# MLP unit 0's gate in two pieces, and the query fold over six blocks of 120 rows loaded later

## The chip, the cores and the metric

The kernel runs on one core of one Trainium2 chip. The metric is the device time of one execution in microseconds (us), as the median of several runs. The engines are TensorE (PE, with its weight loads shown apart as PEld), VectorE (DVE), ScalarE (ACT), GpSimd (POOL) and SyncE (SP, which here only issues DMAs).

## What is computed

The input x has 2048 tokens of 640 features. It is normalised (layernorm), and two branches read the normalised xn: a linear attention with 32 heads of 20 features, and a gated MLP with 1536 hidden features. The output is x + attention + MLP.

```python
qkv = (xn @ wqkv)                      # 640 -> 3 x 640, split in 32 heads of 20
pq, pk = q @ w_phi, k @ w_phi          # per head 20 x 20
phi_q = concat(softmax(pq), softmax(-pq)); phi_k likewise
kv = phi_k^T v;  z = sum(phi_k)        # per head, over all tokens
o  = (phi_q kv) / (phi_q z + 1e-6);  A = o @ wo
h  = silu(xn @ w1) * (xn @ w3);  B = h @ w2
out = x + A + B
```

## The kernel before

The tokens are 16 tiles of 128. A tile t is normalised in place in `x_tok` and transposed into `xnT` (features on the partitions, tokens along the free axis). Tiles 0 to 3 are transposed on PE with an identity matrix (`xn_transpose`), tiles 4 to 15 by DMA transposes that SP issues (`loads`), one of 160 KB for each tile.

The feature map is folded into the projections. Wqp is wq times a block-diagonal matrix that holds w_phi for each head, and Wkp is the same with wk; with them xn @ Wqp gives pq at once. For the fold, wq and wk stand transposed in `wqkT` (five chunks of 128 rows each, one chunk list for wq and one for wk). Each is brought by one DMA transpose of 640x640 from DRAM. The block-diagonal chunks `BDc` are made on POOL from `phi_s` and the mask `GM`. 128 rows aren't a whole number of heads of 20, so a chunk touches 7 or 8 heads and neighbouring chunks overlap by one head; `fold_mm` makes one output chunk `dc` of Wqp or Wkp in six matmuls of 140, 140, 80, 80, 140 and 140 columns, which accumulate into two PSUM banks of 320 columns. The fold of wk (`which` = 1) runs between 17 and 20 us of the profile, the fold of wq (`which` = 0) as one `fold_mm` after each of the token tiles 9 to 13.

The MLP is 48 units (`mlp`): unit n = 12 b + fc takes the 512 tokens of block b and 128 hidden features. A unit is five matmuls for the gate (w1), five for the up-projection (w3), each 128x128 weights on 512 tokens, a tanh on ACT, and two DVE operations. Attention takes each tile's keys (`k_tile`: ten matmuls of 320 columns, two exponentials) and its values (`v_tile`). Then come the key norms, the key-value sums, the queries, and the output tiles (`outs`), which add both branches.

The order of all instructions is made by a planner before the program is built. There are 14 streams (`norms`, `transposes`, `fold_k`, `attention`, `k_norms`, `loads`, `key_values`, ..., `mlps`, `outs`); each yields its next step, or None while a condition on the table `done` doesn't hold. The planner keeps a clock for each engine (`P.free`), a cost for every instruction and a landing time for every DMA, and in each turn commits the step that can start first by these counts; on a tie the stream that stands earlier in the list wins, so `attention` goes ahead of `mlps`. For a step with PE work the start is the larger of PE's free time + 0.15 and the time at which its inputs are there (`P.ready`), to which 0.25 (`SLACK`) is added after 20 us. What comes out is a fixed list for each engine; on the chip every engine works its list in order and waits on semaphores. A DMA transpose of less than 500 KB counts as 1.28 us of SP and lands, if no earlier transfer holds it back, 0.5 us + its bytes at 280 GB/s + 1.6 us after its issue begins; a plain DMA counts as 0.45 us of SP:

```python
if "T" == o.part:
    self.free[o.eng] = t + (1.28 if o.cost < 5e5 else o.cost / 105e3)
self.bus = max(self.bus, t + 0.5) + o.cost / (280e3 if o.part else 305e3)
```

SP's list before: the first loads (x tiles 0 to 3, part of wv, the first third of w1 and w3), `phi_s`, the transpose of wk, x tiles 4 to 15 in three loads, the transpose of wq, then the DMA transposes of tiles 4 to 7, the second third of w1 and w3, the transposes of tiles 8 to 15, the last third of w1 and w3, wo. All PE, ACT, DVE and POOL instructions show as line L102 and all DMA issues as L114, so the text goes by tile names: `w_s` stands for w1, w2 and w3, `t` for t1, `v` for v2.

Of the kernel before, what the change touches and what calls it, by code (L numbers as in the profile page):

```python
# [3 lines left out]
ACT = mybir.ActivationFunctionType  # L4
ALU = mybir.AluOpType
# [4 lines left out]
D = 640  # L10
H = 32
DH = 20
# [237 lines left out]
def bass_parallel_sum__linear_kernel_hedgehog__glu_gated_swiglu__prompt_kernel(  # L250
# [37 lines left out]
    GM = new("GM", [128, DC, H], bf)  # L288
    phi_s = new("phi_s", [128, DC, DH], bf)
    BDc = new("BDc", [128, DC, 8 * DH], bf)  # L290
    bst = new("bst", [128, T, 15], f32)
    mv = new("mv", [128, T, 2], f32)
    rstd = new("rstd", [128, T, 2], f32)
# [25 lines left out]

    RE = region(T * 2 * D * 2 + 96)  # L320
    ekt = new("ekt", [128, T * 2 * D + 48], bf, RE)
    hT3 = new("hT3", [128, FC, 512], bf, RE)
    w2_s = new("w2_s", [128, FC, D], bf, RE + 12288)
    eq = [new(f"eq{i}", [128, NG * 128], bf, (RKV, RE + 27648)[i // 2] + 2816 * (i % 2)) for i in range(4)]
# [5 lines left out]
    oT = new("oT", [128, DC, S], bf, RV)  # L330

    RW = region(12800)
    wqkT = new("wqkT", [128, 2 * DC, D], bf, RW)
    KVc = new("KVc", [128, NG * 64], bf, RW)
    half = new("half", [128, 2, 660], f32, RW + 1408)
    Sq = new("Sq", [128, 4, 72], f32, RW + 6688)
# [55 lines left out]
    def memset(eng, o, v):  # L392
        P.op(eng, "memset", [o], [], (o, v), cost=0.15 + free(o) / 960)
# [8 lines left out]
    out_t = out.rearrange("b (t p) d -> p (b t) d", p=128)  # L402
    wqkv_t = A_wqkv.rearrange("(c p) n -> p c n", p=128)
    phi_t = A_w_phi.rearrange("h d f -> (h d) f").rearrange("(c p) f -> p c f", p=128)
    w1_t = B_w1.rearrange("(c p) f -> p c f", p=128)
    w3_t = B_w3.rearrange("(c p) f -> p c f", p=128)

# [7 lines left out]
    def first_loads():  # L415
        def part_wv(eng, a, b):
            P.dma(eng, wv[:, :, a:b], wqkv_t[:, :, 2 * D + a:2 * D + b])

        P.dma("SP", x_tok[:, 0, 0:320], x_t[:, 0, 0:320])
        P.dma("ACT", x_tok[:, 1, :], x_t[:, 1, :])  # L420
        P.dma("SP", x_tok[:, 0, 320:D], x_t[:, 0, 320:D])
        load_x(2, 3)
        part_wv("ACT", 0, VCUT)
        part_wv("SP", VCUT, D)
        load_x(3, 4)
        w13(0, 512)
        P.dma("SP", phi_s[:], phi_t)
        P.dma("SP", wqkT[:, DC:2 * DC, :], A_wqkv[:, D:2 * D], True)
        load_x(4, 8)
        load_x(8, 12)  # L430
        load_x(12, 16)
        P.dma("SP", wqkT[:, 0:DC, :], A_wqkv[:, 0:D], True)


    def consts():
        memset("DVE", t1[:, 2, 0:128], 0.0)
        memset("DVE", warm[:], 0.0)
        memset("DVE", bst[:, :, 12:14], 0.0)
        memset("DVE", bst[:, :, 14:15], D * EPS)
        act(warm[:], warm[:], ACT.Exp)  # L440
        memset("POOL", ident[:], 0.0)
        select(ident[:], 0, [[-1, 128]], 1, ALU.not_equal, 1.0)
        memset("POOL", GM[:], 1.0)
        select(GM[:], 0, [[128, DC], [-DH, H]], 1, ALU.is_ge, 0.0)
        select(GM[:], DH, [[-128, DC], [DH, H]], -1, ALU.is_gt, 0.0)
        memset("POOL", mhalf[:], -0.5)
        memset("POOL", M3[:, 0:3], 1.0)
        select(M3[:, 0:3], 0, [[-40, 3]], 1, ALU.is_ge, 0.0)
        select(M3[:, 0:3], 40, [[40, 3]], -1, ALU.is_gt, 0.0)
        memset("POOL", ekt[:, T * 2 * D:T * 2 * D + 48], 1.0)  # L450
# [77 lines left out]
               phi_s[:, c, :].unsqueeze(1).to_broadcast([128, n, DH]),  # L528
               GM[:, c, h0:h1 + 1].unsqueeze(2).to_broadcast([128, n, DH]), ALU.mult)

    def fold_mm(which, dc, k, eng=None):
        first = [True, True]
        for e in range(DC):
            h0, h1 = heads_of_chunk(e)
            lo, hi = DH * h0, DH * (h1 + 1)
            for q in range(2):
                a, b = max(lo, 320 * q), min(hi, 320 * q + 320)
                if a < b:
                    mm(bank(k + q, b - a, a - 320 * q), wqkT[:, which * DC + e, 128 * dc:128 * dc + 128],
                       BDc[:, e, a - lo:b - lo], first[q], e == DC - 1 or (q == 0 and e == 2), True)  # L540
                    first[q] = False
        dst = (Wqp, Wkp)[which]
        o = dst[:, dc, :].rearrange("p (b c) -> p b c", c=320)
        if eng:
            copy(eng, o, bank2(k, 320))
        else:
            evac(o, bank2(k, 320))
# [134 lines left out]
    def mlp(b, fc, k, cut=DC, dc=None):  # L682
        n = nmlp[0] % 3
        nmlp[0] += 1
        for w, kk in ((w1_s, k), (w3_s, k + 1)):
            for i in range(DC):
                if kk > k and i == cut:
                    held.add(k // 2)
                    fold_mm(1, dc, banks(2), "ACT")
                    held.discard(k // 2)  # L690
                mm(bank(kk), w[:, i, fc * 128:(fc + 1) * 128], xnT[:, i, b * 512:(b + 1) * 512],
                   i == 0, i == DC - 1)
            if kk == k:
                act(th[:, n, :], bank(k), ACT.Tanh, 0.5)
                stt(t1[:, n, :], th[:, n, :], 1.0, bank(k), ALU.add, ALU.mult)
        stt(hT[b][:, fc, :], t1[:, n, :], 0.5, bank(k + 1), ALU.mult, ALU.mult)

    finish = []

# [31 lines left out]
                       default=0.0)  # L731
        return min((k for k in range(0, 8, n) if k // 2 not in held), key=free_at)

    done = dict.fromkeys(("w", "ln", "t", "f", "k", "n", "kv", "v", "u", "qp", "qn", "qd", "q", "o", "h", "v0", "bd"), 0)

    def norms():
        yield lambda: (first_loads(), consts())
        yield lambda: act_sum(1, ACT.Copy, mv[:, 1, 0:1], scale=-1.0 / D)
        yield lambda: (ln_half(0, 0), ln_half(0, 1), ln_rstd(0, 1))
        yield lambda: act_sum(1, ACT.Square, mv[:, 1, 1:2], mv[:, 1, 0:1])  # L740
        yield lambda: (ln_apply(0, 0, 256), ln_apply(0, 256, D))
        done["ln"] = 1
        yield lambda: act_rstd(1)
        yield lambda: (ln_half(2, 0), ln_half(2, 1))
        yield lambda: ln_apply(1)
        done["ln"] = 2
        yield lambda: ln_rstd(2, 1)
        while done["t"] < 2:
            yield None
        yield lambda: ln_apply(2)  # L750
        done["ln"] = 3
        yield lambda: (ln_half(3, 0), ln_half(3, 1), ln_rstd(3, 1))
        yield lambda: ln_apply(3)
        done["ln"] = 4
        while done["t"] < 4:
            yield None
        yield lambda: memset("DVE", v_heads(v2[:].rearrange("p t n -> p (t n)"))[:, :, :, DH], 1.0)
        yield block_diag
        done["bd"] = 1
        todo = []  # L760
        for t in range(4, T + 2, 2):
            if t == T or t > done["k"] + 8:
                for u in todo:
                    yield lambda u=u: ln_apply(u)
                    done["ln"] = u + 1
                todo = []
            if t == T:
                break
            while t > done["k"] + 8:
                yield None  # L770
            yield lambda t=t: ln_stats(t, 2)
            for u in todo:
                yield lambda u=u: ln_apply(u)
                done["ln"] = u + 1
            todo = [t, t + 1]

    def fold_k():
        while done["u"] < 2:
            yield None
        for dc in range(1, DC - 1):  # L780
            yield lambda dc=dc: fold_mm(1, dc, banks(2), "ACT")
        done["f"] = 1

    done["w"] = 4
# [22 lines left out]
    def loads():  # L807
        while done["t"] < 4:
            yield None
        for t in range(4, T):  # L810
            while done["ln"] <= t:
                yield None
            yield lambda t=t: P.dma("SP", xnT[:, :, t * 128:(t + 1) * 128], x_tok[:, t, :], True)
            done["t"] = t + 1
            if t == 7:
                yield lambda: w13(512, 1024)
                done["w"] = 8
        yield lambda: w13(1024, 1536)
        done["w"] = 12

    def attention():
# [4 lines left out]
        for t in range(4):  # L826
            while done["t"] <= t:
                yield None
            k = banks(2)
            held.add(k // 2)  # L830
            for q in range(2):
                for i in range(DC):
                    if t == 0 and q == 1:
                        while done["t"] < 2:
                            yield None
                    yield lambda t=t, q=q, i=i, k=k: v_part(t, q, i, k)
                    done["v0"] += 1
            yield lambda t=t, k=k: v_store(t, k)
            held.clear()
        while done["u"] < 3:  # L840
            yield None
        for t in range(T):
# [4 lines left out]
            if t >= 4:  # L847
                yield v(t)
            if 9 <= t < 14:
                yield lambda dc=t - 9: fold_mm(0, dc, banks(2))  # L850
        yield lambda: P.dma("SP", wo_s[:], A_wo.rearrange("(c p) d -> p c d", p=128))
        done["v"] = 1

# [60 lines left out]
    CUTS = {1: (3, 0), 2: (0, DC - 1)}  # L914

    def mlps():
        for b in range(NB):
            for fc in range(FC):
                while done["t"] < 4 * b + 4 or done["w"] <= fc or b == 2 and done["t"] < T or b == 3 and not done["kv"]:
                    yield None  # L920
                n = 12 * b + fc
# [122 lines left out]
```

## Time and profile before

| what | value |
| --- | --- |
| median of 3 runs | 268.06 us (267.88 to 269.06) |
| profiled execution, its own time | 268.03 us |
| its span, first to last instruction | 266.3 us |
| PE busy | 261.8 us (98%) |
| DVE, ACT, POOL busy | 169.2, 98.3, 97.9 us |
| granted TensorE clock | 1.000 |

The span leaves out about 1.7 us of the execution's own time. A matmul's record has a modelled end, so busy PE time says when PE had work, and the spacing of matmuls is read from the starts in the timeline. Some matmul records are missing. The profile's rows that carry the argument stand in the prediction.

### The profile page before, as it was taken

To read this page: it belongs to the slowest core of one execution; us is meant where nothing else is said; L and a number is where in the kernel's file an instruction comes from. 1 tells how busy PE (TensorE), PEld (TensorE's weight loads), DVE (VectorE), ACT (ScalarE), POOL (GpSimd) and SP (SyncE) were. 2 spreads that over 40 slices of the span, in tenths; PEclk is the share of its full clock that TensorE was granted. 3 is DMA by queue.
4 is the path that set the end of the run, shared out by engine and by line. 5 is a ranking of instruction groups with operands and counts; after the bars stand their busy time and mean duration, and the time that the engine had idled before them with its cause. 6 is when DMAs were issued, how large, how long until landed. Compare 5 with 4: busy or idle time off the path is not lost.

```text
span 266.3 us, 4843 instructions
## 1 busy us (share of the span) xinstructions
PE 261.8 (98%) x1962; PEld 161.9 (61%) x1981; DVE 169.2 (64%) x293; ACT 98.3 (37%) x196; POOL 97.9 (37%) x136
## 2 busy tenths in 40 slices
PE   8999999999999999999999999999999999999996
PEld 7666777775444575455545555554677777777773
DVE  4469989974998957769788888888723121212112
ACT  5578998878222206344344333442100000000000
POOL 4313459999461332734265544444200000000000
PEclk9999999999999999999999999999999999999999
DMA  7999896600007059247335356365422412131211
GB/s 224 279 319 195 121 252 158 240 2 0 0 0 111 0 157 242 54 55 106 79 79 81 80 99 109 84 70 93 101 67 84 102 58 89 52 98 52 85 38 49
DMA packets 63510, 27.73 MB, mean 104 GB/s; under 512 B 50560, under 2 KB 63488, under 8 KB 63488
## 3 DMA queue, kind: packets, MB, share of 16 engines
q1 hardware_dynamic: 62544, 26.66, 44.2%
q10 hardware_dynamic: 944, 0.77, 0.9%
q8 instruction: 15, 0.25, 0.4%
q14 instruction: 7, 0.06, 0.1%
HBM read 12.81 MB, written 2.62 MB: 58 GB/s over the span
## 4 chain that ended last, share of the span: by engine, by line
PE 98%; issue 0%; DVE 0%
PE PS L102 98%; DVE xres L102 0%; DVE t L102 0%; DVE bst L102 0%; DVE warm L102 0%
## 5 line engine op out<-in xcount | busy, mean ns | idle before, releaser
L102 PE MATMUL PS<-xnT,w_s 128*128 128x512 bf16 x466 | 105.5, 379 | 0.9 <-issue 0.2
L102 PEld LDWEIGHTS PS<-xnT,w_s 128*128 128x128 bf16 x480 | 45.9, 98 | 51.4 <-ACT xnT L102 0.3
L102 PE MATMUL PS<-w_s,hT 128*128 128x320 bf16 (+2 forms) x384 | 54.9, 299 | 0.0
L102 DVE TENSOR_TENSOR xres<-PS,xres 128x640 bf16<-128x640 f32 (+2 forms) x17 | 13.4, 786 | 57.7 <-PE PS L102 57.7
L102 ACT ACTIVATE th<-PS 128x512 f32<-128x512 f32 x48 | 29.2, 609 | 51.4 <-PE PS L102 51.4
L102 POOL TENSOR_TENSOR ekt<-ekt,rS 128x640 bf16<-128x640 bf16 x32 | 39.5, 1272 | 19.8 <-DVE rS L102 19.8
L102 PEld LDWEIGHTS PS<-w_s,hT 128*128 128x128 bf16 x384 | 37.1, 98 | 15.1
L102 DVE SCALAR_TENSOR_TENSOR t<-th,PS 128x512 bf16<-128x512 f32 x48 | 32.6, 679 | 17.5 <-ACT th L102 16.8
L102 DVE SCALAR_TENSOR_TENSOR hT<-t,PS 128x512 bf16<-128x512 bf16 x48 | 33.0, 688 | 5.4 <-DVE t L102 0.5
L102 ACT ACTIVATE eq<-PS 128x600 bf16<-128x600 f32 (+1 forms) x72 | 23.7, 424 | 27.9 <-PE PS L102 27.9
L102 PE MATMUL PS<-wv,xnT 128*128 128x320 bf16 (+2 forms) x160 | 24.6, 300 | 0.0
L102 PE MATMUL PS<-wo_s,oT 128*128 128x320 bf16 (+2 forms) x159 | 24.3, 299 | 0.1
L102 PE MATMUL PS<-Wkp,xnT 128*128 128x320 bf16 x160 | 23.7, 299 | 0.0
L102 PE MATMUL PS<-Wqp,xnT 128*128 128x512 bf16 (+1 forms) x156 | 23.3, 297 | 0.2
L102 DVE TENSOR_REDUCE S<-ekt 128x64 f32<-128x1280 bf16 x16 | 23.0, 1440 | 0.0
L102 POOL TENSOR_TENSOR eq<-eq,rq 128x600 bf16<-128x600 bf16 (+1 forms) x32 | 22.6, 728 | 1.2
L102 ACT ACTIVATE ekt<-PS 128x640 bf16<-128x640 f32 x32 | 20.5, 705 | 3.6 <-PE PS L102 3.6
L102 POOL TENSOR_TENSOR half<-eq 128x660 f32<-128x660 bf16 x14 | 19.0, 1357 | 4.4 <-ACT eq L102 4.4
L102 POOL TENSOR_TENSOR rq<-rq,Sq 128x32 f32<-128x32 f32 x16 | 4.0, 253 | 44.6 <-DVE rq L102 40.5
L102 PEld LDWEIGHTS PS<-wv,xnT 128*128 128x128 bf16 x160 | 15.3, 98 | 6.5 <-ACT xnT L102 0.4
L102 PEld LDWEIGHTS PS<-wo_s,oT 128*128 128x128 bf16 x160 | 15.4, 98 | 6.2
L102 PEld LDWEIGHTS PS<-Wqp,xnT 128*128 128x128 bf16 x160 | 12.8, 98 | 10.2
(57 smaller groups left out, 180.5 us busy)
## 6 DMA issues: line engine op xcount, KB each, us to landing
w_s<-in_B_w_dram SPq DMA_DIRECT2D x6, 640.0 KB, 6.0
xres<-in_A_x_dram SPq DMA_DIRECT2D x16, 160.0 KB, 2.4
out_dram<-xres SPq DMA_DIRECT2D x15, 160.0 KB, 1.8
x_tok<-in_A_x_dram SPq DMA_DIRECT2D x3, 640.0 KB, 6.0
w_s<-in_B_w_dram SPq DMA_DIRECT2D x1, 1920.0 KB, 7.6
wo_s<-in_A_wo_dram SPq DMA_DIRECT2D x1, 800.0 KB, 7.1
wv<-in_A_wqkv_dram ACTq DMA_DIRECT2D x1, 560.0 KB, 5.0
x_tok<-in_A_x_dram SPq DMA_DIRECT2D x2, 160.0 KB, 4.7
```

Source lines behind the costliest of these rows:

```text
L102: o = _Op(eng, lambda: m(*args, **kw), r, w, cost)
```

## The change

Three things change together.

1. MLP unit 0 is no longer one step. Its gate is computed for the first 384 tokens as soon as three tiles are transposed (`mlp_first`), and for the last 128 tokens, with the rest of the unit, once the fourth is (`mlp_rest`). The pair of PSUM banks is held in between.
2. The query fold takes six blocks of rows at a stride of 120 (six whole heads; the last block has 40 rows of use, two heads). wq is loaded transposed in six DMA transposes of 128 columns of wqkv each (`load_wqT`); the last 8 rows of each block are not used. The block-diagonal matrix for it is `BD6`, made on POOL in one operation after unit 0 (`block_diag6`) from `phi_6`, which two more small loads bring, and the mask `GM6`. `fold_q` makes one output chunk in six matmuls: five of 120 columns and one of 40, contracting over 120 rows, into 640 contiguous PSUM columns.
3. The transposed wq is no longer loaded at the start behind the x tiles. Three of the six loads are issued behind the DMA transpose of tile 9 and three behind that of tile 11. The fold after tile 9 may not be planned before the second three are in the plan (`done["wq"]`). wk's transposed copy moves to another place in the memory, and the loads of `phi_6` stand ahead of x tiles 4 to 15 in SP's list.

```diff
+    GM6 = new("GM6", [128, 6], bf)
+    phi_6 = new("phi_6", [128, 6, DH], bf)
+    wkT = new("wkT", [128, DC, D], bf, RE + 20480)
-    wqkT = new("wqkT", [128, 2 * DC, D], bf, RW)
+    wqT = new("wqT", [128, 6, D], bf, RW)
+    BD6 = new("BD6", [128, 6, 120], bf, RW + 7680)
@@ first_loads
+        memset("POOL", phi_6[:, 5, :], 0.0)
...
         P.dma("SP", phi_s[:], phi_t)
-        P.dma("SP", wqkT[:, DC:2 * DC, :], A_wqkv[:, D:2 * D], True)
+        P.dma("SP", wkT[:], A_wqkv[:, D:2 * D], True)
+        P.dma("SP", phi_6[0:120, 0:5, :], phi_r[0:600, :].rearrange("(c p) f -> p c f", p=120))
+        P.dma("SP", phi_6[0:40, 5, :], phi_r[600:D, :])
         load_x(4, 8)
         load_x(8, 12)
         load_x(12, 16)
-        P.dma("SP", wqkT[:, 0:DC, :], A_wqkv[:, 0:D], True)
+
+    def load_wqT(a, b):
+        for g in range(a, b):
+            P.dma("SP", wqT[:, g, :], A_wqkv[:, 120 * g:120 * g + 128], True)
@@ consts
+        memset("POOL", GM6[:], 1.0)
+        select(GM6[:], 0, [[-DH, 6]], 1, ALU.is_ge, 0.0)
+        select(GM6[:], DH, [[DH, 6]], -1, ALU.is_gt, 0.0)
@@ the folds
+    def block_diag6():
+        o = BD6[0:120].rearrange("p c (h f) -> p c h f", f=DH)
+        tt("POOL", o, phi_6[0:120].unsqueeze(2).to_broadcast([120, 6, 6, DH]),
+           GM6[0:120].unsqueeze(1).unsqueeze(3).to_broadcast([120, 6, 6, DH]), ALU.mult)
+
+    def fold_q(dc, k):
+        c0 = k * 512 + 32
+        for g in range(6):
+            n = 120 if g < 5 else 40
+            mm(PS[:, c0 + 120 * g:c0 + 120 * g + n], wqT[0:120, g, 128 * dc:128 * dc + 128],
+               BD6[0:120, g, 0:n], g in (0, 4), g in (3, 5), True)
+        evac(Wqp[:, dc, :], PS[:, c0:c0 + D])
+
-    def fold_mm(which, dc, k, eng=None):
+    def fold_mm(dc, k, eng=None):
@@ the MLP
+    def mlp_first(k, lo, hi):
+        for i in range(DC):
+            mm(bank(k, hi - lo, lo), w1_s[:, i, 0:128], xnT[:, i, lo:hi], i == 0, i == DC - 1)
+
+    def mlp_rest(k):
+        mlp_first(k, 384, 512)
+        n = nmlp[0] % 3
+        nmlp[0] += 1
+        act(th[:, n, :], bank(k), ACT.Tanh, 0.5)
+        stt(t1[:, n, :], th[:, n, :], 1.0, bank(k), ALU.add, ALU.mult)
+        for i in range(DC):
+            mm(bank(k + 1), w3_s[:, i, 0:128], xnT[:, i, 0:512], i == 0, i == DC - 1)
+        stt(hT[0][:, 0, :], t1[:, n, :], 0.5, bank(k + 1), ALU.mult, ALU.mult)
@@ norms
         yield block_diag
         done["bd"] = 1
+        while done["u"] < 1:
+            yield None
+        yield block_diag6
@@ loads, inside the loop over tiles
+            if t in (9, 11):
+                yield lambda a=(t - 9) // 2 * 3: load_wqT(a, a + 3)
+                done["wq"] = t // 11
@@ attention
-            held.clear()
+            held.discard(k // 2)
...
             if 9 <= t < 14:
-                yield lambda dc=t - 9: fold_mm(0, dc, banks(2))
+                while not done["wq"]:
+                    yield None
+                yield lambda dc=t - 9: fold_q(dc, banks(2))
@@ mlps
+        while done["t"] < 3 or not done["w"]:
+            yield None
+        k = banks(2)
+        held.add(k // 2)
+        yield lambda: mlp_first(k, 0, 384)
+        while done["t"] < 4:
+            yield None
+        yield lambda: mlp_rest(k)
+        held.discard(k // 2)
+        done["u"] = 1
         for b in range(NB):
-            for fc in range(FC):
+            for fc in range(1 if b == 0 else 0, FC):
```

More of the change, by code (lines that the diff above doesn't have):

```diff
@@ L404, in bass_parallel_sum__linear_kernel_hedgehog__glu_gated_swiglu__prompt_kernel @@
     phi_t = A_w_phi.rearrange("h d f -> (h d) f").rearrange("(c p) f -> p c f", p=128)
+    phi_r = A_w_phi.rearrange("h d f -> (h d) f")
     w1_t = B_w1.rearrange("(c p) f -> p c f", p=128)
@@ L538, in fold_mm @@
                 if a < b:
-                    mm(bank(k + q, b - a, a - 320 * q), wqkT[:, which * DC + e, 128 * dc:128 * dc + 128],
+                    mm(bank(k + q, b - a, a - 320 * q), wkT[:, e, 128 * dc:128 * dc + 128],
                        BDc[:, e, a - lo:b - lo], first[q], e == DC - 1 or (q == 0 and e == 2), True)
                     first[q] = False
-        dst = (Wqp, Wkp)[which]
-        o = dst[:, dc, :].rearrange("p (b c) -> p b c", c=320)
+        o = Wkp[:, dc, :].rearrange("p (b c) -> p b c", c=320)
         if eng:
@@ L688, in mlp @@
                     held.add(k // 2)
-                    fold_mm(1, dc, banks(2), "ACT")
+                    fold_mm(dc, banks(2), "ACT")
                     held.discard(k // 2)
@@ L732, in banks @@
         return min((k for k in range(0, 8, n) if k // 2 not in held), key=free_at)
-    done = dict.fromkeys(("w", "ln", "t", "f", "k", "n", "kv", "v", "u", "qp", "qn", "qd", "q", "o", "h", "v0", "bd"), 0)
+    done = dict.fromkeys(("w", "ln", "t", "f", "k", "n", "kv", "v", "u", "qp", "qn", "qd", "q", "o", "h", "v0", "bd", "wq"), 0)
     def norms():
@@ L780, in fold_k @@
         for dc in range(1, DC - 1):
-            yield lambda dc=dc: fold_mm(1, dc, banks(2), "ACT")
+            yield lambda dc=dc: fold_mm(dc, banks(2), "ACT")
         done["f"] = 1
```

## The prediction

> **What bounds the kernel now.** I read the page's busy times first, then the waits of PE, then the timeline of PE, its weight loads and SP for the first 60 us.
>
> ```profile
> PE 261.8 (98%) x1962; PEld 161.9 (61%) x1981; DVE 169.2 (64%) x293; ACT 98.3 (37%) x196; POOL 97.9 (37%) x136
> PEclk9999999999999999999999999999999999999999
> PE PS L102 <- DVE bst L102: 1.1, 1, 1.1
> PE PS L102 <- issue: 0.2, 1, 0.2
> ```
>
> The first line gives busy time and share, the second the granted clock in 40 slices, the last two what PE waited for in the whole span: 1.1 us ahead of its first matmul, and 0.2 us once. So PE is the bound, at full clock, and stands still for nothing behind it. A change can gain what it takes off PE's own list, and it loses whatever wait it puts there, one for one.
>
> The 0.2 us is ahead of MLP unit 0, where PE waits for tile 3's transposed x:
>
> ```profile
> 11.43 0.41 PE L102 MATMUL PS<-wv,xnT 128*128 128x192 bf16 x3
> 11.80 0.11 PEld L102 LDWEIGHTS PS<-xnT,w_s 128*128 128x128 bf16 x2 [0.19 <-DVE xnT L102]
> 12.03 2.11 PE L102 MATMUL PS<-xnT,w_s 128*128 128x512 bf16 x9 [0.20 <-issue]
> 13.97 1.52 PE L102 MATMUL PS<-wv,xnT 128*128 128x448 bf16 x10
> 15.33 1.89 PE L102 MATMUL PS<-xnT,w_s 128*128 128x512 bf16 x8
> 17.06 0.48 PE L102 MATMUL PS<-BDc,wqkT 128*128 128x140 bf16 x6
> ```
>
> Columns: start, length, what, count, idle time before it. Eight matmuls of 512 columns from 15.33 to 17.06 are spaced 0.216 us. Unit 0 has ten, and only nine have a record: counted back from 13.97 the first stood at 11.81, right behind its weights at 11.80. The three matmuls before it, of 192 columns, are spaced 0.083 (half of the row's 0.41 is the modelled tail), and end at 11.67. The real gap is 0.14 us.
>
> **Part 1, the split gate.** Tiles 0 to 2 are there by then, so 384 columns of gate fill the gap: minus 0.14. The matmuls are five more, but hold the same columns. By these rows
>
> ```profile
> 7.71 0.44 PE L102 MATMUL PS<-ident,x_tok 128*128 128x128 bf16 x5
> 7.99 1.14 PE L102 MATMUL PS<-wv,xnT 128*128 128x192 bf16 x8
> 41.62 1.52 PE L102 MATMUL PS<-wv,xnT 128*128 128x320 bf16 x10
> 42.98 0.48 PE L102 MATMUL PS<-BDc,wqkT 128*128 128x140 bf16 x6
> 43.30 1.52 PE L102 MATMUL PS<-Wkp,xnT 128*128 128x320 bf16 x10
> 100.22 0.48 PE L102 MATMUL PS<-KVc,eqT 128*128 128x63 bf16 x11
> 100.54 0.81 PE L102 MATMUL PS<-Wqp,xnT 128*128 128x512 bf16 x3
> ```
>
> 128 columns take 0.28/5 = 0.056 us, 320 take 1.36/10 = 0.136; 384 lie between at 0.162. So 0.218 instead of 0.216: plus 0.01 for five. If w1 came late the gap would stay; the nearest bound is that nothing is gained, 0. I take minus 0.13.
>
> **Part 2, the fold's matmuls.** A fold takes 43.30 - 42.98 = 0.32 us. New: five of 120 columns at 0.056 x 120/128 = 0.053 and one of 40, for which the 63-column matmuls (0.32/11 = 0.029) stand: 0.29. Five folds gain 0.15 at most and, if the spacing doesn't shrink, 0; I take minus 0.12. The evacuation still moves 640 columns. `block_diag6` is one POOL operation of 720 elements; the nearest row
>
> ```profile
> L102 POOL TENSOR_TENSOR ekt<-ekt,rS 128x640 bf16<-128x640 bf16 x32 | 39.5, 1272 | 19.8 <-DVE rS L102 19.8
> 20.77 0.70 POOL L102 TENSOR_TENSOR rstd<-mv,mhalf 128x2 f32<-128x2 f32 x1 [6.58 <-DVE mv L102]
> ```
>
> has 640 elements in 1.27 us, so about 1.4 us. It falls into the 6.58 us in which POOL is idle ahead of tile 4's rstd and costs nothing; if `phi_6` came after 19.4 it would push that rstd, and tile 4 with it. GM6's and `phi_6`'s few memory-filling operations lie on POOL before 4.7, where it waits for DVE anyway.
>
> **Part 3, the loads, and here the time is decided.** SP's list:
>
> ```profile
> 4.28 2.24 SPq L114 DMA_DIRECT2D phi_s<-in_A_w_phi_dram  x1
> 6.56 6.33 SPq L114 DMA_TRANSPOSE wqkT<-in_A_wqkv_dram  x1
> 12.94 1.67 SPq L114 DMA_DIRECT2D x_tok<-in_A_x_dram  x3
> 14.66 7.53 SPq L114 DMA_TRANSPOSE wqkT<-in_A_wqkv_dram  x1
> 23.04 5.75 SPq L114 DMA_TRANSPOSE xnT<-x_tok  x4
> 28.84 2.21 SPq L114 DMA_DIRECT2D w_s<-in_B_w_dram  x2
> 31.09 11.84 SPq L114 DMA_TRANSPOSE xnT<-x_tok  x8
> 42.97 0.58 SPq L114 DMA_DIRECT2D w_s<-in_B_w_dram  x1
> DMA to landing us min/median/max: 9.5/9.8/10.0
> DMA to landing us min/median/max: 2.5/3.2/4.2
> ```
>
> (The last two rows are the views of `wqkT` in the whole span and of `xnT` for the issues from 34.8 to 40.3.) Before, wq's transpose lay between 14.66 and 22.2, when SP had no tile to transpose, and landed at 14.66 + 9.5 = 24.2, 19 us ahead of its use at 42.98. Now it lies in the middle of tiles 8 to 15. SP needs 6.33/5 = 1.27 us for five blocks of 128x128, which is also what it needs for one x tile, so each new load costs an x tile's place. The last of the six is the tenth issue from 31.09 (tiles 8 and 9, three, tiles 10 and 11, three). Eight take until 42.97; two more at 1.32 end at 45.6. From the end of the issue to the landing, wq took 9.5 - 7.5 = 2.0 us, wk 10.0 - 6.3 = 3.6, the x tiles at best 2.5 - 1.3 = 1.2. So wq is complete at 46.8 to 49.2; I take wq's own 2.0: 47.6.
>
> PE comes to the first query fold at 42.98 - 0.13 = 42.85. How it fills the time until then is the planner's doing. Its count for a DMA transpose of this size is 1.28 us of SP and a landing 0.5 + 0.585 + 1.6 = 2.7 us after the issue begins, so from 31.09 the last is issued at 42.6 and there at 45.3; with the 0.275 of the five matmuls ahead of the one that needs it, its 0.07 and the slack of 0.25 the fold can start at 45.3. At 42.85 MLP unit 3 can start sooner and is put in, 2.16 us, to 45.01. Then the fold and unit 4 compete: unit 4 wins if PE's time + 0.15 is below 45.3. On the chip's clock that is 45.16. But the planner's costs, followed through from the start, count w3 and so the key tiles some 0.4 us later than the chip (no time of mine is taken from them); by its own clock it is about 45.5, both streams tie, and attention goes first. So I expect one unit in the gap. The SP list then meets the chip's real issue times, which the planner counts too short: the three transposes behind the w1/w3 loads take
>
> ```profile
> L114 SPq DMA_TRANSPOSE xnT<-x_tok x3: 1444/1575/2126, 31.1 to 34.8; - x3
> ```
>
> 1.44, 2.13 and 1.58 us, not 1.28. PE stands at 45.01 and waits until 47.6: a wait of 2.6 us (1.8 to 4.2). Behind it in PE's list are the keys of tile 10 and everything after; ACT and DVE run out of fresh keys. The fold then runs 47.6 to 47.89, and tile 10's keys start there instead of at 43.30, with 2.16 us of unit 3 done ahead: 47.89 - 43.30 - 2.16 = plus 2.43. The four later folds give back 4 x 0.03. Net plus 2.3. The gain of part 1 is swallowed, since the wait ends at a landing.
>
> The other things on SP: `phi_6`'s two loads stand ahead of x tiles 4 to 15. `phi_s`, the same 40-byte rows, held SP 2.24 us; 640 rows again, so 0.9 (two ordinary issues of about 0.45) to 2.5 us with a second issue of 0.4. x tile 4 landed at 12.94 + 5.0 = 17.9 behind wk; now it is 17.9 to 19.2 (15.5 + 0.6 of issue + 3.1), and its statistics started at 18.64. So 0 to 0.6 us on the chain that prepares tile 4:
>
> ```profile
> 18.64 1.80 DVE L102 BATCH_NORM_STATS2 bst<-x_tok 128x6 f32<-128x320 bf16 x4
> 26.67 1.20 PEld L102 LDWEIGHTS PS<-Wkp,xnT 128*128 128x128 bf16 x10 [0.18 <-DMA xnT<-x_tok]
> L114 SPq DMA_TRANSPOSE xnT<-x_tok x1: 1202/1202/1202, 23.0 to 23.0; - x1
> DMA to landing us min/median/max: 3.6/3.6/3.6
> ```
>
> Tile 4 landed at 23.04 + 3.6, just when its weights were wanted. With wq gone from the DMAs it should take nearer 2.9 (the median of tiles 5 to 7), so the two cancel: 0 to 0.4 us of PE wait, taken as 0, since the fold's wait covers it. If the whole chain slips, the tenth issue slips by up to 0.5 as well; that widens the range. The last third of w1/w3 and wo move 8 us later, to a landing below 60; the units that need them come after 63 and the outputs after 189: nothing.
>
> **A rule of the Trainium skill on this step.** Above, SP's issue of 1.27 us for 160 KB sets the pace. The Trainium skill, "DMA: Bandwidth & Descriptors", section "Latency and other measured facts", gives DMA transposes an effective 261 GB/s with a non-contiguous middle dimension. An estimate by that page would be 0.63 us a load, 3.8 us for six, and no wait left. The trace doesn't agree: 800 KB of wk held SP for 6.33 us, 129 GB/s.
>
> **The rivals.**
>
> B: the planner puts in a second unit (4). For it: by the chip's clock it would win by 0.18 us. Against it: the planner's own clock. PE then reaches the fold at 47.17 and waits 0 to 0.4 us: 268.03 + 0.43 - 0.12 - 0.2, about 268.1. It decides from the point at which the planner counts the landing past PE's time + 0.15.
>
> C: the wait is hidden altogether, because the six small loads issue faster than an x tile's 1.27 us, 0.85 or less (end at 43.0, landing at 45.0). Then only the terms of parts 1 and 2 are left, 268.03 - 0.13 - 0.12 = 267.8. Both rows of wqkT speak against it.
>
> D: more is lost: no unit fits in, a wait of 4.8 us and 272.5; or the late landing of 49.2 with one unit, 271.9; or later transposes of queries and outputs come late in the new order, which the trace doesn't price.
>
> E: weights on 120 instead of 128 partitions load slower. The slowest spacing of any 128-column pair here is the warm-up's,
>
> ```profile
> 1.05 4.66 PE L102 MATMUL PS<-t 128*128 128x128 bf16 x42 [1.05 <-DVE bst L102]
> ```
>
> 4.66/42, about 0.11 us; thirty such cost 30 x (0.11 - 0.053) = 1.7 us more. No row has 120 rows of weights. The Trainium skill, "TensorE: Matmul & The Clock Gate", section "LDWEIGHTS (loading the stationary operand)", says that the load goes by its columns and not by the contraction, which speaks against E; no run here shows it yet.
>
> **How the numbers follow.** This profiled execution took 268.03 us, 0.03 below the median of the runs, so its sums need no correction. A measurement of this kernel can tell 0.5% (1.3 us) from no change. The likeliest: one unit and a wait, 268.03 + 2.3 = 270.3, its own range 269.5 (landing 46.8) to 271.4; chance 0.58. B 0.22, C 0.08, D 0.09, E on top of B 0.03. Slower by over 0.5% (above 269.4) are nearly all of the first, D, and E: 0.64. Faster by over 0.5% needs 1.3 us, and parts 1 and 2 hold 0.3: 0.02. The rest, 0.34, is within. The range takes in B and all but C's edge: 267.9 to 271.4.
>
> **What would show it.** In the profile after: PE's wait ahead of the first fold on BD6, put down to DMA wqT or as a hole near 45 us, of 1.8 to 4.2 us; nine or ten matmuls of one unit right before it; the sixth wqT transpose issued at 44 to 45; wqT's issues about 1.3 us each; folds of 0.29 us; unit 0's gate right behind tile 2's values with no gap. Two units before the fold, or wqT issues below 0.9 us, make the forecast wrong to the fast side; holes elsewhere in PE's list to the slow side.

## The result, and the profile after

The changed kernel takes 270.48 us (270.05 to 271.35), the kernel before 268.02 beside it: the ratio is 1.0093, with a 95% interval of 1.0077 to 1.0110. It is slower by 2.5 us. The profiled execution took 270.26 us, with a span of 268.5.

The first fence is from the page of the changed kernel and from its view of PE's waits: busy times, then what PE waited for in the whole span (us in total, times, the longest).

```profile
PE 263.2 (98%) x1986; PEld 161.9 (60%) x1986; DVE 169.4 (63%) x293; ACT 98.1 (37%) x196; POOL 99.8 (37%) x141
PE PS L102 <- DMA wqT<-in_A_wqkv_dram: 1.4, 2, 0.9
PE PS L102 <- DVE bst L102: 1.1, 1, 1.1
PE PS L102 <- DMA xnT<-x_tok: 0.5, 1, 0.5
```

The wait ahead of the first matmul is as before. The one ahead of MLP unit 0 is gone, and two new ones stand in its place, both on DMA transposes: the wq loads and an x tile. The next fence is the timeline of PE, from the third tile's values to the second query fold (start, length, what, idle time before it).

```profile
11.22 0.41 PE L102 MATMUL PS<-wv,xnT 128*128 128x192 bf16 x3
11.47 0.98 PE L102 MATMUL PS<-xnT,w_s 128*128 128x384 bf16 x5
...
20.89 7.19 PE L102 MATMUL PS<-Wkp,xnT 128*128 128x320 bf16 x50
...
36.07 1.52 PE L102 MATMUL PS<-wv,xnT 128*128 128x320 bf16 x10
38.07 1.52 PE L102 MATMUL PS<-Wkp,xnT 128*128 128x320 bf16 x10 [0.48 <-DMA xnT<-x_tok]
...
43.51 2.32 PE L102 MATMUL PS<-xnT,w_s 128*128 128x512 bf16 x10
45.66 0.38 PE L102 MATMUL PS<-BD,wqT 120*128 120x120 bf16 x4
46.55 0.23 PE L102 MATMUL PS<-BD,wqT 120*128 120x120 bf16 x1 [0.51 <-DMA wqT<-in_A_wqkv_dram]
47.66 0.19 PE L102 MATMUL PS<-BD,wqT 120*128 120x40 bf16 x1 [0.88 <-DMA wqT<-in_A_wqkv_dram]
47.76 1.52 PE L102 MATMUL PS<-Wkp,xnT 128*128 128x320 bf16 x10
...
50.47 0.45 PE L102 MATMUL PS<-BD,wqT 120*128 120x120 bf16 x6
50.76 1.52 PE L102 MATMUL PS<-Wkp,xnT 128*128 128x320 bf16 x10
```

Read by the starts, with 0.136 us for a matmul of 320 columns, three holes are to be seen. The 50 key matmuls of tiles 0 to 4 last from 20.89 to 27.92, 7.03 us, where 50 x 0.136 is 6.8: 0.23 us of wait inside, at tile 4, for whose transposed x the weight load waits 0.40 us. Tile 7's values end at 37.43 and tile 8's keys begin at 38.07: 0.64. The first fold lasts from 45.66 to 47.76, 2.10 us, the second from 50.47 to 50.76, 0.29: 1.81. One MLP unit, ten matmuls of 512 columns, stands ahead of the first fold. Behind it PE has no hole, as before.

SP's list of the changed kernel, and the landing of the last two wq loads (view of `wqT` for the issues from 42.8 to 44.1):

```profile
30.99 3.01 SPq L114 DMA_TRANSPOSE xnT<-x_tok  x2
34.05 4.71 SPq L114 DMA_TRANSPOSE wqT<-in_A_wqkv_dram  x3
38.80 2.60 SPq L114 DMA_TRANSPOSE xnT<-x_tok  x2
41.44 3.90 SPq L114 DMA_TRANSPOSE wqT<-in_A_wqkv_dram  x3
L114 SPq DMA_TRANSPOSE wqT<-in_A_wqkv_dram x2: 1272/1272/1272, 42.8 to 44.1; - x2
DMA to landing us min/median/max: 3.5/3.6/3.7
```

The sixth load is issued at 44.07 and lands 3.5 us later, at 47.6. The fold's last matmul starts at 47.66.

### The profile page after: what moved, and what is told of

The parts are those of the page before. It is cut to its first block, busy times and chain, and to the rows that moved or that the text cites. A ratio compares the mean times of both kernels' runs of the same rounds, so it can differ in the third digit from the quotient of the medians.

```text
span 268.5 us, 4883 instructions
## 1 busy us (share of the span) xinstructions
PE 263.2 (98%) x1986; PEld 161.9 (60%) x1986; DVE 169.4 (63%) x293; ACT 98.1 (37%) x196; POOL 99.8 (37%) x141
## 2 busy tenths in 40 slices
DMA packets 64975, 27.92 MB, mean 104 GB/s; under 512 B 52025, under 2 KB 64953, under 8 KB 64953
## 4 chain that ended last, share of the span: by engine, by line
PE 85%; DVE 9%; DMA 1%; SPq 1%; issue 1%; ACT 1%; POOL 0%; DVEq 0%; ACTq 0%
PE PS L102 85%; DVE bst L102 4%; DVE S L102 2%; DMA wqT<-in_A_wqkv_dram 1%; SPq L114 1%; DVE hT L102 1%; DVE x_tok L102 1%; DVE t L102 1%; DVE rS L102 1%; DVE mv L102 1%; ACT v L102 0%; POOL rstd L102 0%; DVE v L102 0%; ACT th L102 0%; ACT xnT L102 0%
## 5 line engine op out<-in xcount | busy, mean ns | idle before, releaser
L102 PE MATMUL PS<-xnT,w_s 128*128 128x512 bf16 (+2 forms) x485 | 107.7, 377 | 0.0
L102 PE MATMUL PS<-Wqp,xnT 128*128 128x512 bf16 (+1 forms) x160 | 24.2, 299 | 0.0
L102 PEld LDWEIGHTS PS<-Wkp,xnT 128*128 128x128 bf16 x160 | 15.1, 98 | 6.9 <-ACT ekt L102 0.8
```

Of the source, the lines that this page charges most:

```text
L102: o = _Op(eng, lambda: m(*args, **kw), r, w, cost)
```

## The experiments

All times below are medians; "before" is the kernel before, run on the same chip beside them (267.94 to 267.97). Where a profiled execution is summed up, the sum starts from 268.03, the profiled execution before, and takes 0.25 us off for parts 1 and 2 where the kernel has both.

### Is it the place of the loads? The six loads at the start

```diff
         load_x(12, 16)
+        load_wqT(0, 6)
...
-            if t in (9, 11):
-                yield lambda a=(t - 9) // 2 * 3: load_wqT(a, a + 3)
-                done["wq"] = t // 11
...
-                while not done["wq"]:
-                    yield None
```

> The six loads of wq back at the start, behind x tiles 4 to 15; the split gate and the six-block fold stay. Theory (the loss is PE's wait for the sixth wq load, which lands at 47.6 in the middle of the x tiles' transposes): no MLP unit and no wait ahead of the first query fold, wq landed by about 26, time 267.7 to 268.3, ratio to the kernel before 0.999 to 1.001. Rival (the loss sits in the new fold or the two small loads, whatever the place of the wq loads): still above 269.5. The chain of tiles 4 and 8 may still keep PE waiting 0.2 to 0.8 us, since PE comes there earlier.

272.41 us, ratio 1.018 (1.015 to 1.021): even slower. The fold's wait is gone, as the theory says, but the time isn't back, as the rival says. For tiles 4 and 8 I had allowed 0.2 to 0.8 us of wait; it was far more at tile 4. PE's waits, PE's timeline and SP's list of this run:

```profile
PE PS L102 <- DMA xnT<-x_tok: 3.1, 2, 2.6
PE PS L102 <- DMA wv<-in_A_wqkv_dram: 1.0, 1, 1.0
30.26 1.53 PE L102 MATMUL PS<-Wkp,xnT 128*128 128x320 bf16 x10 [2.56 <-DMA xnT<-x_tok]
47.22 0.45 PE L102 MATMUL PS<-BD,wqT 120*128 120x120 bf16 x6
16.86 10.62 SPq L114 DMA_TRANSPOSE wqT<-in_A_wqkv_dram  x6
27.53 6.10 SPq L114 DMA_TRANSPOSE xnT<-x_tok  x4
```

At the start one large transpose of wq took SP 7.5 us and was done at 22.2, just ahead of tile 4. Six loads take 10.62, so tile 4's transpose is issued at 27.53 instead of 23.04 (some 1.2 us of this is a late start of SP's list in this execution), and PE waits 2.6 us for it. (The wait for wv is at the start of the profiled execution; the profiles of the kernel before and of the changed kernel don't have it.) So the early place isn't free for six loads. The wait isn't all of the loss: the profiled execution had a mean clock of 1.000, but three of the other five had 0.994 (271.9 to 272.4 us) and two 0.987 (274.4 us). The last section comes back to this.

The same six loads at the start, with the gate whole:

> The six-block fold alone, with its six loads at the start and the gate whole. Theory: a fold takes 0.29 us instead of 0.32, five save 0.12 to 0.15 us, POOL's one operation for the block-diagonal matrix is hidden: 267.9. Rival (weights on 120 partitions load slower, or the small loads push the x tiles): folds longer than 0.32 us, or a wait of over 0.3 us ahead of tile 4's keys, 268.3 or more.

272.7 us, 1.018 (1.013 to 1.022), where the theory had 267.9. A fold takes 0.29 us (the first from 49.63 to 49.92), like the later folds of the changed kernel; the loss begins with the same wait, 3.78 us for tile 4 in the profiled execution. What a lower clock adds to it there is in the last section.

To see whether the late tiles cost at one place or at each, MLP unit 3 was put between the keys of tiles 3 and 4 of the first of these two kernels:

```diff
             while done["t"] <= t or t == 4 and done["u"] < 4:
                 yield None
             yield lambda t=t: k_tile(t, banks(2))
```

> The six loads of wq at the start, as in the first experiment, with MLP unit 3 ahead of tile 4's keys. Theory (at the start the six loads hold SP until 27.5 instead of 22.2, so the transposes of tiles 4 to 8 come some 4 us later, and PE's waits of 2.7 and 0.65 us there are all of that run's loss): 2.16 us of work go into the first wait, 0.5 us of it stay, the second stays at about 0.65, no drop of the clock: 268.03 - 0.25 + 1.15 = 268.9. Rival (the late tiles delay PE at each tile, not at two): 270.5 or more.

270.02 us, 1.009 (1.006 to 1.012), between the two forecasts, so the trace has to decide. PE has one hole left, ahead of tile 4's keys; tiles 5 to 8 wait for nothing.

```profile
26.29 2.32 PE L102 MATMUL PS<-xnT,w_s 128*128 128x512 bf16 x10
30.46 1.53 PE L102 MATMUL PS<-Wkp,xnT 128*128 128x320 bf16 x10 [1.85 <-DMA xnT<-x_tok]
```

268.03 - 0.25 + 2.0 = 269.8, and the profiled execution took 269.57. So it is one place, but my 0.5 us there was too low: I had taken it from the first run, whose PE began tile 0's keys at 22.10 instead of 20.85, after the wait for wv.

### Is it the number of units in the gap? Two units ahead of the fold

```diff
-                while not done["wq"]:
+                while not done["wq"] or done["u"] < 5:
                     yield None
```

> The changed kernel, with the first query fold held in the plan until MLP units 3 and 4 are both ahead of it. Theory (one unit too few in the gap, and the wait for the sixth load swallows the 0.2 and 0.65 us that PE waits for tiles 4 and 8 before): the fold starts at about 47.8, its wait is 0 to 0.2 us, the waits for tiles 4 and 8 now count, 268.03 - 0.25 + 0.85 = 268.6, so 1.8 us below the changed kernel. Rival 1 (only the wait at the fold counts, the early ones cost nothing): 267.9. Rival 2 (the loads' place costs PE otherwise, by contention or a late tile 10 to 15): the wait comes back elsewhere and the time stays above 269.8.

269.11 us, 1.0043 (1.0027 to 1.0058), 1.4 us below the changed kernel. PE's waits and its timeline:

```profile
PE PS L102 <- DMA wqT<-in_A_wqkv_dram: 0.4, 1, 0.4
PE PS L102 <- DMA xnT<-x_tok: 0.4, 1, 0.4
43.56 4.48 PE L102 MATMUL PS<-xnT,w_s 128*128 128x512 bf16 x20
47.88 0.43 PE L102 MATMUL PS<-BD,wqT 120*128 120x120 bf16 x5
48.74 0.19 PE L102 MATMUL PS<-BD,wqT 120*128 120x40 bf16 x1 [0.44 <-DMA wqT<-in_A_wqkv_dram]
48.84 1.52 PE L102 MATMUL PS<-Wkp,xnT 128*128 128x320 bf16 x10
```

The fold now lasts 0.96 us, so 0.67 of wait are left; the sixth load landed at about 48.7 here, 1.1 us later than in the changed kernel: it was issued at 44.41 and held SP for 2.10 us instead of 1.27, for a reason that wasn't separated. With that, and 0.26 and 0.57 us at tiles 4 and 8, the sum is 269.3, the profiled execution 269.22. The theory holds, with the landing off by a microsecond. Neither rival does: the early waits count here, and no other wait came up.

### Do the earlier waits count? The one unit ahead of tile 4

The unit is moved from the front of the fold to the front of tile 4's keys (the edit shown above), and unit 4 is held until the first fold:

```diff
                 yield lambda dc=t - 9: fold_q(dc, banks(2))
+                done["f"] = 2
...
-                while n == 1 and not done["bd"] or n == 2 and not done["f"]:
+                while n == 1 and not done["bd"] or n == 2 and not done["f"] or n == 4 and done["f"] < 2:
```

> The changed kernel with its one unit, number 3, moved from the front of the first query fold to the front of tile 4's keys, and unit 4 held back until that fold. Theory (the wait at the fold ends at the landing of the sixth load, so what PE waits before doesn't count): the waits of 0.2 and 0.65 us for tiles 4 and 8 are gone, PE comes to the fold at 45.0, waits 2.6 us or more, and the time is that of the changed kernel, 270.2 to 270.8. Rival (the waits add up): 269.6.

271.18 us, 1.012 (1.009 to 1.015); the profiled execution took 270.56, within the 270.2 to 270.8 expected. The median is above that: two of the six executions had a mean clock of 0.994 and took 272.2 and 272.4 us, and two at 1.000 took 271.2.

```profile
PE PS L102 <- DMA wqT<-in_A_wqkv_dram: 2.4, 2, 1.3
44.88 0.42 PE L102 MATMUL PS<-BD,wqT 120*128 120x120 bf16 x4
46.39 0.23 PE L102 MATMUL PS<-BD,wqT 120*128 120x120 bf16 x1 [1.08 <-DMA wqT<-in_A_wqkv_dram]
47.96 0.19 PE L102 MATMUL PS<-BD,wqT 120*128 120x40 bf16 x1 [1.34 <-DMA wqT<-in_A_wqkv_dram]
48.06 1.52 PE L102 MATMUL PS<-Wkp,xnT 128*128 128x320 bf16 x10
```

The waits for tiles 4 and 8 are gone, the fold starts at 44.88 and ends at 48.06: 3.18 us, 2.89 of them waiting, 1.08 more than in the changed kernel. PE came to the fold 0.78 us earlier, and the load landed 0.30 later. So the early waits of the changed kernel cost nothing by themselves: the wait at the fold ends at a landing.

### Does the place alone cost? One large load behind tile 11

The kernel before, with only its one transpose of wq moved into `loads`, behind tile 11, and the fold held until it is planned:

```diff
-        P.dma("SP", wqkT[:, 0:DC, :], A_wqkv[:, 0:D], True)
...
+            if t == 11:
+                yield lambda: P.dma("SP", wqkT[:, 0:DC, :], A_wqkv[:, 0:D], True)
+                done["wq"] = 1
```

> The kernel before, with nothing changed but the place of wq's one large transpose: behind the transpose of tile 11 instead of at the start. The planner counts this load at 7.8 us of SP and puts MLP units 3 and 4 ahead of the first fold. Theory (the late place costs only what the units in the gap don't cover): the load is issued at about 37.7 to 44, lands at 46 to 47.6, PE comes to the fold at 47.3, wait 0 to 0.4 us, 268.0 to 268.5. Rival (the place itself costs, through later tiles 12 to 15 or through contention): 269.5 or more.

268.08 us, 1.0006 (0.9991 to 1.0020): no difference. PE's timeline, SP's list and the load's time to landing:

```profile
43.66 4.48 PE L102 MATMUL PS<-xnT,w_s 128*128 128x512 bf16 x20
47.97 0.48 PE L102 MATMUL PS<-BDc,wqkT 128*128 128x140 bf16 x6
38.58 4.06 SPq L114 DMA_TRANSPOSE wqkT<-in_A_wqkv_dram  x1
DMA to landing us min/median/max: 6.9/6.9/6.9
```

The load, issued at 38.58, lands at 45.5, and two units put PE at the fold at 47.97. So the place costs nothing with two units ahead, which the plan's count of 7.8 us for this load puts there. The run differs from the changed kernel in one more thing, the number of loads: one load held SP for 4.06 us, the six for 4.71 + 3.90, and it landed 2.1 us earlier than the sixth did at 47.6. By an estimate from these rows even one unit would have brought PE to the fold at 45.8, behind the landing. So the late landing comes of the place and of the six small loads together, and not of the place alone.

### The parts alone, and all with their cover

The split gate alone:

> The kernel before with the split gate alone. Theory: the gap of 0.14 us ahead of MLP unit 0 is gone; tiles 4 and 8 land when they did, just in time before, so part of it comes back as a wait there: 267.9 to 268.1, not told from the kernel before by time, but by the trace: no gap at 11.7, a wait of 0 to 0.2 us ahead of the keys of tile 4 or 8. Rival (the gain stays): 267.85 and no wait.

268.35 us, 1.0010 (1.0000 to 1.0020), above the 267.9 to 268.1 expected; the profiled execution took 268.13. In the trace the gap at 11.7 is gone, and PE waits for tile 4 instead:

```profile
11.29 0.41 PE L102 MATMUL PS<-wv,xnT 128*128 128x192 bf16 x3
11.54 0.98 PE L102 MATMUL PS<-xnT,w_s 128*128 128x384 bf16 x5
26.74 1.53 PE L102 MATMUL PS<-Wkp,xnT 128*128 128x320 bf16 x10 [0.19 <-DMA xnT<-x_tok]
```

With MLP unit 3 ahead of tile 4's keys:

> The kernel before with the split gate, and MLP unit 3 held in the plan between the keys of tile 3 and of tile 4. Theory (the gate's gain is given back at tile 4, whose transpose lands just in time): with 2.16 us of work ahead of it PE waits for neither tile 4 nor tile 8, and the gain stays: 267.8 to 267.9, 0.3 to 0.5 below the split gate alone. Rival (the split gate itself costs what it gains): as the split gate alone, 268.3.

267.99 us, 0.9998 (0.9983 to 1.0012), 0.36 below the gate alone, and PE waits for nothing after its first matmul; the profiled execution took 267.66. So the trace agrees with the theory; by the times the gain can't be told from the kernel before, and the two intervals, with and without unit 3, overlap.

The whole change, with unit 3 ahead of tile 4's keys and units 4 and 5 ahead of the first fold:

```diff
-                while not done["wq"]:
+                while not done["wq"] or done["u"] < 6:
                     yield None
```

> The changed kernel with all its parts, MLP unit 3 ahead of tile 4's keys and units 4 and 5 ahead of the first query fold. Theory (all of the loss is PE waiting for three landings, and there is work to put ahead of each): PE reaches the fold at 49.3, after the sixth load, no waits for tiles 4 and 8: 267.8 to 268.0, ratio 0.999 to 1.000, 2.5 us below the changed kernel. Rival (something else in the change costs, a later transpose or POOL): 268.6 or more with no wait at the three places.

267.75 us, 1.0000 (0.9979 to 1.0021); the profiled execution took 267.61, 0.42 below that of before.

```profile
26.36 2.32 PE L102 MATMUL PS<-xnT,w_s 128*128 128x512 bf16 x10
44.82 4.48 PE L102 MATMUL PS<-xnT,w_s 128*128 128x512 bf16 x20
49.13 0.45 PE L102 MATMUL PS<-BD,wqT 120*128 120x120 bf16 x6
49.43 1.52 PE L102 MATMUL PS<-Wkp,xnT 128*128 128x320 bf16 x10
```

The fold takes 0.30 us; the sixth load landed at 48.6, ahead of it. The changed kernel's median is 2.7 us above this one, and that is gone with three MLP units in other places and not a single matmul less. So nothing else in the change costs time that can be measured. Whether this version beats the kernel before isn't settled: its median is lower by 0.2 us, and the interval holds 1.

## Why the prediction was right, and where it was not

It said 270.3 us, in a range of 267.9 to 271.4, and slower by over 0.5%; measured are 270.48 us and 0.93%.

**What was right.** PE was the bound, and the loss is PE's wait for the sixth wq load. The planner put one unit into the gap (that it did so because two streams tied on its clock, as I argued, isn't shown). The load was issued at 44.07 ("at 44 to 45") and landed at 47.6 (47.6). Tile 10's keys began at 47.76 (47.89). That the wait swallows the waits ahead of it is shown by the run with the unit ahead of tile 4. The folds took 0.29 us, and unit 0's gate followed tile 2's values with no gap. The block-diagonal matrix took POOL 1.39 us (1.4), from 16.30, ahead of tile 4's rstd:

```profile
16.30 1.39 POOL L102 TENSOR_TENSOR BD<-phi,GM 120x720 bf16<-120x720 bf16 x1 [2.56 <-DMA phi<-in_A_w_phi_dram]
20.80 0.70 POOL L102 TENSOR_TENSOR rstd<-mv,mhalf 128x2 f32<-128x2 f32 x1 [3.11 <-DVE mv L102]
```

**What was luck.** That the landing came out to a tenth is partly luck. SP was done with the sixth load at 45.34 and not at 45.6, and the landing came 2.2 us behind that and not 2.0; the two errors cancel. Ahead of it tiles 8 and 9 took SP less than I had counted and the first three wq loads more. In the other runs with the loads at this place the sixth landed between 47.9 and 48.7.

**What was off.** I expected PE at the fold at 45.01 and a wait of 2.6 us there. PE came at 45.66 and waited 1.8, at the low edge of what I said, because 0.23 us had been waited at tile 4 and 0.64 at tile 8; against that, the profiled execution was 0.21 us ahead of the one before by 11.2 us. For tile 4 I had 0 to 0.4 us, on the ground that its transpose would land nearer 2.9 us after its issue with wq gone; it took 3.4 (3.6 before). Tile 8 isn't in my working at all: it landed 6.9 us after its issue instead of 6.1. In the changed kernel this is hidden; in the run with two units it counts. Rival B was priced at 268.1 without it and measured 269.1. The wq loads behind tile 8 aren't shown to be what delays it: with them it took 6.4 to 7.0 us in four profiles, and without them, in the three profiles with the six loads at the start and in both with the split gate and no other part, 6.0 to 6.8.

The two small loads held SP for 0.61 + 0.38 us, the low end of what I gave them, and tile 4's transpose was issued at 23.06 (23.04 before); `phi_s`, with the same rows, took 1.62 and 2.24 in the two profiles, so its 2.24 is no price of 40-byte rows. One reading of the working is loose: the modelled tail of the row of 0.41 us is 0.16, what three spacings of 0.083 leave of it, and not half; the gap of 0.14 us stands.

Part 1's 0.13 us is a gain only where tile 4 doesn't take it back. I had said so for the changed kernel, because of the fold's wait; in the trace of the gate alone it is also so without it.

Rival E is refuted: 30 weight loads of 120 rows (view of `wqT`) took as long as those of 128 rows in the kernel before, where the view of `wqkT` gave 97 to 99 ns.

```profile
L102 PEld LDWEIGHTS PS<-BD,wqT x30: 95/97/100, 45.5 to 59.7; 120*128 120x128 bf16 x30
```

The Trainium skill, "TensorE: Matmul & The Clock Gate", section "LDWEIGHTS (loading the stationary operand)", says that a weight load's time goes by its columns and not by the contraction. The two measurements agree.

## What to carry to other kernels

Where one engine is the bound and has no holes, a moved load costs what its landing passes the point at which that engine needs it, and independent work put ahead of that point in the list makes this smaller; so look for work that can be moved there before looking for a faster load. An order made from a planner's costs is only as good as its counts of issue and landing: six loads at 1.28 us each looked covered by one unit, and on the chip PE waited 1.8 us for the last. A gain ahead of a transfer that lands just in time is given back at that transfer. And clearing one wait can bring up the next: two units cleared most of the fold's wait and made those of tiles 4 and 8 count.

## What the runs showed of the hardware

**The SP time of a DMA transpose isn't fixed by its size.** A 640x640 transpose of 800 KB held SP for 6.33 (wk) and 7.53 us (wq) at the start of the kernel before, and that of wq for 4.06 us behind tile 11. Six loads with 30 blocks together took 4.71 + 3.90 = 8.6 us in the middle and 10.58 to 11.17 in three profiles with all six at the start. That x tiles were still landing there (until 23.5 us in the run where the six took 10.62) may be the cause; it wasn't separated.

**A long wait can cost twice.** In the run with the six-block fold alone, PE waited 3.78 us for tile 4 and then ran at half the clock for 6 us. Its windows (us, PE busy, granted clock, DMA share, GB/s) and its timeline:

```profile
28.00:30.00 2.00, 0.00 (x0) 0.87 0.89 141
30.00:36.00 6.00, 5.51 (x21) 0.50 0.83 108
30.49 2.85 PE L102 MATMUL PS<-Wkp,xnT 128*128 128x320 bf16 x10 [3.78 <-DMA xnT<-x_tok]
...
38.76 1.52 PE L102 MATMUL PS<-Wkp,xnT 128*128 128x320 bf16 x10
```

The ten matmuls of 320 columns from 30.49 last 2.85 us, those from 38.76 1.52. The wait cost 3.9 us and the clock some 2.8 more: 268.03 - 0.12 + 6.7 = 274.6, and this execution took 274.59. The Trainium skill, "TensorE: Matmul & The Clock Gate", section "Part 1: The HAM clock gate (the "warmup" mystery)", says that the clock halves after an idle window of about 3.4 us and that the windows run freely. The trace agrees with the half clock behind 3.78 us.

The drop doesn't come in every execution. Of the six of this kernel, two had a mean clock of 1.000 and took 271.1 and 271.4 us, two had 0.994 and took 272.4 and 273.0, and two, the profiled one among them, had 0.987 and took 274.6 and 274.7. With all six loads at the start and the split gate, the profiled execution waited 2.56 us at a mean clock of 1.000, and the five others had 0.994 or 0.987. Where the profiled waits were shorter still, 1.85 us at one place (unit 3 ahead of tile 4) or 1.08 and 1.34 us in one fold (the unit moved from the fold to tile 4), two of seven and two of six executions had 0.994, and took some 1.5 us longer than the others. How long PE waited in the executions that weren't profiled isn't known, so the length of wait that is safe isn't shown. In the changed kernel and the five other runs, whose profiles list no wait of 0.9 us or more behind the first matmul, every execution had 0.999 or 1.000.
